# A two-layer MoE behind attention on one core: block 0's load and maximum moved beside the second layer's weights, and a two-instruction activation

## The chip, the cores and the metric

The program runs on one core of a Trainium2 chip. The metric is device microseconds of one execution, lower is better; the time before is the median of three runs. Engines are named as in the profile: PE (TensorE matmuls), PEld (its weight loads), DVE (VectorE), ACT (ScalarE), POOL (GpSimd) and SP (SyncE, which issues every DMA of this kernel).

## The reference, cut to what matters

```python
def _moe_ref(x, w_in, w_out):            # layer 1, after the attention
    h = x @ w_in                         # 1792 x 768 times 768 x 2048
    g = h * (1.0 / (1.0 + np.exp(-1.702 * h)))
    return (g @ w_out).astype(np.float32)

def _moe2_ref(x, w_in, w_out, alpha):    # layer 2
    h = x @ w_in
    g = np.maximum(h, 0.0) + alpha * np.minimum(h, 0.0)
    return (g @ w_out).astype(np.float32)
```

The attention has 4 batches of 12 heads, 448 positions each; its output is the x of layer 1, and y of layer 1 is the x of layer 2. alpha holds 2048 numbers between 0 and 0.3, one for each column of h.

## The kernel before

All large matmuls are done in float16 with each operand split into a high and a low half (three matmuls for one product), so every operand needs a scale, and the scale needs a maximum over the whole tensor or block.

**Layer 1.** Attention and layer 1 are interleaved by batch b = 0 to 3. `moe1(b)` computes 16 blocks `hp` (L672, 18 matmuls each), applies the activation (ACT L680, DVE L681), splits the result into `g` (L124, L125), and `moe1_out` then makes 6 tiles `yp` (L695, 48 matmuls each), which ACT copies to `y` (L703) and SP stores to `y_dram` (L704).

**Weights of layer 2.** While batch 3 runs, `late_weights` steps through `weights(...)`: it loads w_in (`w2raw`), rebuilds its float32 numbers in `w2n` (ACT L132, DVE L148, L149), takes row maxima (L222) and splits the rows into `w2i` (ACT L163, DVE L164). `w2i` lies in the memory of layer 1's `w1i`, which the last `hp` matmul reads. There are four `w2n` tiles for six rows of weights, so the last two rows can be rebuilt only when the first are split. Then the maximum over all rows is taken: `wcol` (L171) on each partition, and `partition_max` across partitions. `partition_max` puts the column on a diagonal (`diag`, L117), multiplies it on PE by a matrix of ones into `pm` (L119), and reduces `pm` on DVE (L120).

**Layer 2.** 1792 tokens are worked in BLOCKS of 512, 512, 512 and 256. `prepare(i)` loads block i of `y_dram` into `yr` (one buffer), takes its maximum (L748), crosses partitions with a `pm` of its own and splits the block into `x2`. `moe2_in(i)` computes 16 blocks `h` (L780, 18 matmuls each), applies the activation and stores `pos` to `g_dram`. Between them `second_out_weights` prepares w_out on ACT and DVE. `token_sums` and `moe2_out` then make the last product (L943).

**What sets the order.** The code issues instructions in one order, and a scheduler with a timeline of its own writes the final order of each engine before the program runs. On the chip each engine works through its own list. `hp`, `yp`, `h` and every `pm` share one PSUM pool, `ps_m`, of three banks, which are also handed out when the order is written. `yr` lies in the pool `p2`, which is opened where the pool `w2s` of the weights was closed. `P0` counts the steps of `late_weights` after which the rest of `prepare(0)` runs; `P1` lists the values of m at which `prepare(i + 1)` goes on.

Of the kernel before, what the change touches and what calls it, by code (L numbers as in the profile page):

```python
# [9 lines left out]
F32 = mybir.dt.float32  # L10
# [3 lines left out]
AF = mybir.ActivationFunctionType  # L14
ALU = mybir.AluOpType
AX = mybir.AxisListType.X
# [29 lines left out]
R1O = 4  # L46
G1I = 1
G1O = 2
P1 = (2, 8)
P0 = 14  # L50
PAIR0 = 44
W2_RAW = 6
RSQRT_SEED = float(0x5F3759DF)
# [3 lines left out]
def attention_moe_kernel(  # L57
# [17 lines left out]
    nc = tc.nc  # L75
# [6 lines left out]
    KD = DM // 128  # L82
    KF = FF // 128
# [3 lines left out]
    const = ctx.enter_context(tc.tile_pool(name="const", bufs=1))  # L87
# [3 lines left out]
    work = ctx.enter_context(tc.tile_pool(name="work", bufs=2))  # L91
# [10 lines left out]
    def pow2floor(dst, src):  # L102

        nc.vector.tensor_scalar(out=dst, in0=src, scalar1=1e-30, scalar2=None, op0=ALU.max)
        nc.vector.tensor_scalar(
            out=dst.bitcast(I32), in0=dst.bitcast(I32), scalar1=EXP_MASK, scalar2=None, op0=ALU.bitwise_and
        )
# [6 lines left out]
    def partition_max(dst, col):  # L114

        diag = small.tile([128, 128], BF16, tag="diag", name="diag", bufs=1)
        nc.vector.tensor_scalar(out=diag, in0=ident, scalar1=col, scalar2=None, op0=ALU.mult)  # L117
        pm = ps_m.tile([128, 128], F32, tag="m", name="pm")
        nc.tensor.matmul(out=pm, lhsT=ones, rhs=diag, start=True, stop=True)  # L119
        nc.vector.tensor_reduce(out=dst, in_=pm, op=ALU.max, axis=AX)  # L120

    def split(dst, src, scale):

        nc.scalar.activation(out=dst[0], in_=src, func=AF.Copy, scale=scale)  # L124
        nc.vector.scalar_tensor_tensor(  # L125
            out=dst[1], in0=src, scalar=scale, in1=dst[0], op0=ALU.mult, op1=ALU.subtract
        )
# [593 lines left out]
    H2 = DM // 2  # L721

    def alpha_scales():

        nalpha = const.tile([128, KF], F32, name="nalpha")
        nc.sync.dma_start(out=nalpha, in_=moe2_alpha.rearrange("(m p) -> p m", p=128))
        am = const.tile([128, 1], F32, name="am")
        nc.vector.tensor_reduce(out=am, in_=nalpha, op=ALU.max, axis=AX, apply_absolute_value=True)
        nc.vector.tensor_scalar(out=am, in0=am, scalar1=1.0, scalar2=None, op0=ALU.max)
        pow2floor(am, am)  # L730
        a2 = const.tile([128, 1], F32, name="a2")
        partition_max(a2, am)
        nc.vector.tensor_scalar(out=nalpha, in0=nalpha, scalar1=-1.0, scalar2=None, op0=ALU.mult)
        ra = const.tile([128, 1], F32, name="ra")
        nc.vector.reciprocal(out=ra, in_=a2)
        return nalpha, a2, ra

    blocks = {}
    w2 = {}

    def prepare(i):

        o, n = BLOCKS[i]
        p2 = w2["p2"]
        yr = p2.tile([128, KD, n], F32, tag="yr", name="yr", bufs=1)
        nc.sync.dma_start(out=yr, in_=y_dram[:, o:o + n].rearrange("(k p) t -> p k t", p=128))
        one = small.tile([128, 1], F32, tag="yone", name="yone")
        nc.vector.tensor_reduce(  # L748
            out=one, in_=yr.rearrange("p k t -> p (k t)"), op=ALU.max, axis=AX, apply_absolute_value=True
        )  # L750
        pow2floor(one, one)
        yield
        my = small.tile([128, 1], F32, tag="my", name="my")
        partition_max(my, one)
        rmy = small.tile([128, 1], F32, tag="rmy", name="rmy")
        nc.vector.reciprocal(out=rmy, in_=my)
        sc = small.tile([128, KD], F32, tag="ysc", name="ysc")
        nc.vector.tensor_scalar(out=sc, in0=scales["w2i"][1], scalar1=rmy, scalar2=None, op0=ALU.mult)
        x2 = [big.tile([128, 2, n], F16, tag="x", name="x2", bufs=NX) for _ in range(KD)]
        for kk in range(KD):  # L760
            split((x2[kk][:, 0], x2[kk][:, 1]), yr[:, kk], sc[:, kk:kk + 1])
        co = const.tile([128, 1], F32, name=f"co{i}")
        nc.vector.tensor_scalar(
            out=co, in0=my, scalar1=scales["w2i"][0], scalar2=2.0 ** -26, op0=ALU.mult, op1=ALU.mult
        )
        blocks[i] = (x2, co)
        yield

    def moe2_in(i, nalpha):

        o, n = BLOCKS[i]
        p2 = w2["p2"]
        w2i = w2["w2i"]
        x2 = blocks[i][0]
        for m in range(KF):
            ps = ps_m.tile([128, n], F32, tag="m", name="h2")
            c = 0
            for kk in range(KD):
                for e, f in ((0, 0), (0, 1), (1, 0)):
                    nc.tensor.matmul(  # L780
                        out=ps, lhsT=w2i[:, kk, e, m * 128:(m + 1) * 128], rhs=x2[kk][:, f], start=(c == 0), stop=(c == 3 * KD - 1)
                    )
                    c += 1
            pos = p2.tile([128, n], F32, tag="pos", name="pos", bufs=3)
            neg = work.tile([128, n], F32, tag="t", name="neg")
            nc.scalar.activation(out=pos, in_=ps, func=AF.Relu)  # L786
            nc.scalar.activation(out=neg, in_=ps, func=AF.Relu, scale=-1.0)  # L787
            nc.vector.scalar_tensor_tensor(  # L788
                out=pos, in0=neg, scalar=nalpha[:, m:m + 1], in1=pos, op0=ALU.mult, op1=ALU.add
            )  # L790
            nc.sync.dma_start(out=g_dram[m * 128:(m + 1) * 128, o:o + n], in_=pos)
            yield
# [173 lines left out]
    def late_weights(ctx, att):  # L966

        att.close()
        with tc.tile_pool(name="w2s", bufs=1) as w2s:

            def w2i():
                if "w2i" not in w2:
                    w2["w2i"] = big.tile([128, KD, 2, FF], F16, tag="w", name="w2i", bufs=2)
                return w2["w2i"]

            yield from weights(
                moe2_w_in, "w2i", w2i, lambda j: w2s.tile([128, FF], F32, tag="num", name="w2n", bufs=4),
                lambda t: w2s.tile([128, 512, 2], I32, tag="raw", name="w2raw", bufs=W2_RAW), 4, W2_RAW, 2.0 ** 13, scales, 2, 4
            )
        w2["p2"] = ctx.enter_context(tc.tile_pool(name="p2", bufs=2))  # L980
        w2["ps"] = ctx.enter_context(tc.tile_pool(name="ps_d", bufs=5, space=bass.MemoryType.PSUM))
        first = prepare(0)
        next(first)
        for _ in range(P0):
            yield
        next(first)
        yield

    def second_layer(late):
        for _ in late:  # L990
            pass
        nalpha, a2, ra = alpha_scales()
        rest = second_out_weights()
        ready = False
        early = token_sums(0)
        step = 0
        for i in range(len(BLOCKS)):
            nxt = prepare(i + 1) if i + 1 < len(BLOCKS) else iter(())
            for m, _ in enumerate(moe2_in(i, nalpha)):
                if m in P1:  # L1000
                    next(nxt, None)
                for _ in range(1 + step % 2):
                    if not ready:
                        ready = next(rest, None) is None and "w2o" in scales
                        if ready:
                            cg = w2["cg"] = const.tile([128, KF], F32, name="cg")
                            nc.vector.tensor_scalar(out=cg, in0=scales["w2o"][1], scalar1=ra, scalar2=None, op0=ALU.mult)
                            nc.vector.tensor_scalar(
                                out=a2, in0=a2, scalar1=scales["w2o"][0], scalar2=2.0 ** 13, op0=ALU.mult, op1=ALU.mult
                            )  # L1010
                if step >= PAIR0:
                    next(early, None)
                step += 1
        for _ in early:
            pass
        obs = w2["p2"].tile([128, 2, 2, 2, H2], F32, tag="yr", name="ob", bufs=1)
        for p in range(NT // 256):
            nxt = token_sums(p + 1)
            next(nxt, None)
            for o, _ in enumerate(moe2_out(p, a2, obs[:, p % 2])):  # L1020
                next(nxt, None)
                next(nxt, None)
            for _ in nxt:
                pass

    if True:
# [51 lines left out]
        steps = attention([4 * P + r for P in range(NP) for r in range(2, 4)])  # L1078
# [26 lines left out]
        for b in range(B):  # L1105
            last = min(NU, 4 * NP * (b + 2)) + LAG
            first = done
# [42 lines left out]
```

## Time and profile before

| | us |
|---|---|
| median of 3 runs | 1219.34 (1214.65 to 1220.08) |
| profiled execution, its own time | 1210.01 |
| its span, first to last instruction | 1208.2 |
| last `hp` matmul of layer 1 ends | 726.91 |
| first `h` matmul of layer 2 starts | 790.06 |

Times within the span count from its start. The profiled execution lies 9.3 us below the median of the runs; 1.8 us of it lie outside the span.

### The profile page before, as it was taken

To read this page: it belongs to the slowest core of one execution; us is meant where nothing else is said; L and a number is where in the kernel's file an instruction comes from. 1 tells how busy PE (TensorE), PEld (TensorE's weight loads), DVE (VectorE), ACT (ScalarE), POOL (GpSimd) and SP (SyncE) were. 2 spreads that over 40 slices of the span, in tenths; PEclk is the share of its full clock that TensorE was granted. 3 is DMA by queue.
4 is the path that set the end of the run, shared out by engine and by line. 5 is a ranking of instruction groups with operands and counts; after the bars stand their busy time and mean duration, and the time that the engine had idled before them with its cause. 6 is when DMAs were issued, how large, how long until landed. Compare 5 with 4: busy or idle time off the path is not lost.

```text
span 1208.2 us, 18626 instructions
## 1 busy us (share of the span) xinstructions
PE 1086.0 (90%) x6829; PEld 610.5 (51%) x6829; DVE 827.2 (68%) x1451; ACT 704.2 (58%) x1447; POOL 138.7 (11%) x236
## 2 busy tenths in 40 slices
PE   0568899868989898999999999799999999999998
PEld 0345577655444444555555545344444467566665
DVE  6999888997555777456751768569895352887451
ACT  3676777877376776567862545237666343665220
POOL 3112000354311513130000000000000000000000
PEclk9878999979999899999999999899999999999999
DMA  7983555577577665666542821364524216244111
GB/s 201 270 213 104 157 134 133 118 149 139 141 150 146 122 146 115 133 123 128 107 88 61 299 92 51 127 251 166 210 79 166 79 66 192 91 148 119 43 27 33
DMA packets 266539, 160.62 MB, mean 133 GB/s; under 512 B 188112, under 2 KB 249808, under 8 KB 266448
## 3 DMA queue, kind: packets, MB, share of 16 engines
q1 hardware_dynamic: 266448, 159.44, 50.3%
q8 instruction: 53, 0.87, 0.3%
q14 instruction: 38, 0.31, 0.1%
HBM read 92.02 MB, written 25.69 MB: 97 GB/s over the span
## 4 chain that ended last, share of the span: by engine, by line
PE 49%; DVE 21%; DMA 12%; ACT 9%; issue 5%; SPq 3%; POOL 0%; DVEq 0%; ACTq 0%
PE op L943 13%; PE yp L695 10%; PE h L780 9%; PE hp L672 7%; PE xp L530 4%; DVE ph L505 3%; ACT pr L461 3%; DMA w2raw<-in_moe_w_in_dram 2%; PE sp L447 2%; DVE nm L452 2%; PE hp L625 2%; DMA vst<-in_v_dram 2%; PE tp L494 2%; DMA yr<-y_dram 1%; DMA w2raw<-in_moe_w_out_dram 1%
## 5 line engine op out<-in xcount | busy, mean ns | idle before, releaser
L695 PE MATMUL yp<-g,w1o 128*128 128x448 f16 x1152 | 229.4, 358 | 4.8 <-DVE g L125 2.6
L780 PE MATMUL h<-x,w2i 128*128 128x512 f16 (+1 forms) x1152 | 219.2, 352 | 3.0 <-ACT neg L787 3.0
L672 PE MATMUL hp<-x,w1i 128*128 128x448 f16 x864 | 169.9, 354 | 2.9 <-DVE t L681 2.9
L695 PEld LDWEIGHTS <-w1o 128*128 128x128 f16 x1152 | 111.5, 99 | 115.7 <-issue 17.7
L780 PEld LDWEIGHTS <-w2i 128*128 128x128 f16 x1152 | 112.6, 98 | 108.5 <-issue 3.7
L505 DVE SCALAR_TENSOR_TENSOR ph<-pr,sm,ph 128x448 f16<-128x448 f32 x126 | 104.9, 857 | 30.9 <-ACT ph L479 30.2
L672 PEld LDWEIGHTS <-w1i 128*128 128x128 f16 x864 | 82.6, 98 | 85.4 <-issue 11.2
L461 ACT ACTIVATE pr<-sp,nm,c_s 128x448 f32<-128x448 f32 x168 | 120.3, 720 | 5.1 <-PE tp L494 3.1
L452 DVE TENSOR_REDUCE nm<-sp 128x2 f32<-128x896 f32 x96 | 92.4, 963 | 8.5 <-PE sp L447 6.4
L479 ACT ACTIVATE ph<-pr,sm 128x448 f16<-128x448 f32 x126 | 78.1, 660 | 22.9 <-DVE sm L470 21.0
L943 PEld LDWEIGHTS <-even 128*128 128x128 f16 x672 | 65.7, 98 | 43.1
L788 DVE SCALAR_TENSOR_TENSOR pos<-neg,nalpha,pos 128x512 f32<-128x512 f32 (+1 forms) x64 | 43.4, 680 | 60.5 <-ACT neg L787 60.3
L447 PE MATMUL sp<-t 64*128 64x448 f16 (+1 forms) x480 | 62.5, 363 | 18.6 <-ACT pr L461 18.6
L625 PE MATMUL hp<-x,w1i 128*128 128x256 f16 (+1 forms) x576 | 64.8, 271 | 11.5 <-DVE t L637 8.0
L786 ACT ACTIVATE pos<-h 128x512 f32<-128x512 f32 (+1 forms) x64 | 34.4, 537 | 67.1 <-PE h L780 58.4
L494 PE MATMUL tp<-dg,pr 128*128 128x128 f32 x336 | 56.1, 326 | 15.4 <-DVE dg L474 14.9
L625 PEld LDWEIGHTS <-w1i 128*128 128x128 f16 x576 | 54.8, 103 | 25.9 <-issue 22.3
L453 ACT ACTIVATE nm<-nm,c_s 128x2 f32<-128x2 f32 x96 | 28.0, 291 | 67.4 <-DVE nm L452 67.3
L943 PEld LDWEIGHTS <-odd 128*128 128x128 f16 x504 | 49.2, 98 | 33.5 <-DVE odd L893 1.1
L943 PE MATMUL op<-w2lo,even 128*128 128x384 f16 x384 | 63.5, 326 | 0.0
L494 PEld LDWEIGHTS tp<-dg,pr 128*128 128x128 f32 x336 | 49.8, 230 | 26.9 <-DVE dg L474 11.8
L125 DVE SCALAR_TENSOR_TENSOR g<-t,ratio_w1o,g 128x448 f16<-128x448 f32 x64 | 45.7, 718 | 18.2 <-ACT g L124 17.9
(202 smaller groups left out, 1620.9 us busy)
## 6 DMA issues: line engine op xcount, KB each, us to landing
g<-in_moe_w_in_dram SPq DMA_DIRECT2D x24, 512.0 KB, 5.0
g<-in_moe_w_out_dram SPq DMA_DIRECT2D x32, 384.0 KB, 3.9
w2raw<-in_moe_w_in_dram SPq DMA_DIRECT2D x24, 512.0 KB, 5.9
w2raw<-in_moe_w_out_dram SPq DMA_DIRECT2D x16, 768.0 KB, 6.4
g_dram<-pos SPq DMA_DIRECT2D x48, 256.0 KB, 2.0
gp<-g_dram SPq DMA_DIRECT2D x8, 1024.0 KB, 6.6
odd<-g_dram SPq DMA_DIRECT2D x6, 1024.0 KB, 5.8
y_dram<-y SPq DMA_DIRECT2D x24, 224.0 KB, 2.4
```

The lines of the kernel that those rows point to most:

```text
L447: nc.tensor.matmul(out=sp[:, j, 0:S] if n == 2 else sp[ds, 0, 0:S], lhsT=qt[ds] if n == 2 else qt[ds, 64:128], rhs=kt[ds, 0:S], start=(i = ...
L452: nc.vector.tensor_reduce(out=nm[:, 0:n], in_=sp[:, 0:n, 0:S], op=ALU.max, axis=AX, negate=True)
L461: nc.scalar.activation(out=pr[i], in_=sp[:, i, 0:S], func=AF.Exp, bias=nm[:, i:i + 1], scale=c_s, accum_out=sm[:, i:i + 1])
L479: nc.scalar.activation(out=ph[:, i, 0:S], in_=pr[i], func=AF.Copy, scale=sm[:, i:i + 1])
L494: nc.tensor.matmul(out=tp[:, c, i], lhsT=pr[i][:, o:o + 128], rhs=ph[:, i], start=True, stop=True)
L505: nc.vector.scalar_tensor_tensor(out=ph[:, i, S:2 * S], in0=pr[i], scalar=sm[:, i:i + 1], in1=ph[:, i, 0:S], op0=ALU.mult, op1=ALU.subtract)
L530: nc.tensor.matmul(out=xp[64 * j:64 * j + 64, t:t + n], lhsT=vs[ks, j, c], rhs=pt[ks, kc, o:o + n], start=(i == 0), stop=(i == len(steps) ...
L625: nc.tensor.matmul(out=ps, lhsT=w1i[:, kk, e, m * 128:(m + 1) * 128], rhs=xs[0, kk][:, f, cols], start=(i == 0), stop=(i == 3 * KD - 1))
L672: nc.tensor.matmul(out=ps, lhsT=w1i[:, kk, e, m * 128:(m + 1) * 128], rhs=x[:, f], start=(n == 0), stop=(n == 3 * KD - 1))
L695: nc.tensor.matmul(out=ps, lhsT=w1o[:, m, e, j * 128:(j + 1) * 128], rhs=g[:, m, f], start=(n == 0), stop=(n == 3 * KF - 1))
L780: nc.tensor.matmul(out=ps, lhsT=w2i[:, kk, e, m * 128:(m + 1) * 128], rhs=x2[kk][:, f], start=(c == 0), stop=(c == 3 * KD - 1))
L943: nc.tensor.matmul(out=ps, lhsT=ops[:, o, m, f], rhs=rhs[:, e], start=(c == 0), stop=(c == 3 * KH - 1))
```

## The change

In layer 2, `yr` gets a pool of its own, `py`, opened as soon as the attention's memory is closed. `prepare(0)` starts there: its load is issued before the weights, its maximum is taken at step 6 of the weights and its `pm` at step 14 (`P0 = (6, 14)`); only the split into `x2` stays behind the weights. `prepare` has more stops, so `P1` has four entries.

The activation changes as well. `sign` is +1 where alpha is at most 1 and -1 elsewhere, `slope` is alpha times sign. ACT writes sign * h, and DVE takes the larger of slope * h and that, reading h from PSUM itself; the sign is multiplied back into `cg`. Before, ACT wrote the relu of h and the relu of -h, and DVE joined the two.

```diff
-P1 = (2, 8)
-P0 = 14
+P1 = (2, 6, 8, 9)
+P0 = (6, 14)
...
-        nalpha = const.tile([128, KF], F32, name="nalpha")
+        slope = const.tile([128, KF], F32, name="slope")
...
+        sign = const.tile([128, KF], F32, name="sign")
+        nc.vector.tensor_scalar(out=sign, in0=slope, scalar1=1.0, scalar2=None, op0=ALU.is_le)
+        nc.vector.tensor_scalar(out=sign, in0=sign, scalar1=2.0, scalar2=-1.0, op0=ALU.mult, op1=ALU.add)
+        nc.vector.tensor_tensor(out=slope, in0=slope, in1=sign, op=ALU.mult)
...
-        nc.vector.tensor_scalar(out=nalpha, in0=nalpha, scalar1=-1.0, scalar2=None, op0=ALU.mult)
...
-        p2 = w2["p2"]
-        yr = p2.tile([128, KD, n], F32, tag="yr", name="yr", bufs=1)
+        yr = w2["py"].tile([128, KD, n], F32, tag="yr", name="yr", bufs=1)
         nc.sync.dma_start(out=yr, in_=y_dram[:, o:o + n].rearrange("(k p) t -> p k t", p=128))
+        yield
...
         nc.vector.reciprocal(out=rmy, in_=my)
+        yield
...
-            neg = work.tile([128, n], F32, tag="t", name="neg")
-            nc.scalar.activation(out=pos, in_=ps, func=AF.Relu)
-            nc.scalar.activation(out=neg, in_=ps, func=AF.Relu, scale=-1.0)
+            nc.scalar.activation(out=pos, in_=ps, func=AF.Copy, scale=sign[:, m:m + 1])
             nc.vector.scalar_tensor_tensor(
-                out=pos, in0=neg, scalar=nalpha[:, m:m + 1], in1=pos, op0=ALU.mult, op1=ALU.add
+                out=pos, in0=ps, scalar=slope[:, m:m + 1], in1=pos, op0=ALU.mult, op1=ALU.max
             )
...
         att.close()
+        w2["py"] = ctx.enter_context(tc.tile_pool(name="py", bufs=1))
+        first = prepare(0)
+        next(first)
...
-            yield from weights(
+            steps = weights(
...
+            for i, _ in enumerate(steps):
+                if i in P0:
+                    next(first)
+                yield
...
-        first = prepare(0)
-        next(first)
-        for _ in range(P0):
-            yield
         next(first)
```

The scheduler wrote a new order on every engine. Three places of it follow.

On PE, at the end of layer 1, the matmul `pm` that carries the maximum of the second layer's weights (its `diag` is made from `wcol`) stood behind three of the six `yp` tiles, `yp_8016` being the third, with 48 matmuls for each tile:

```order
L695 LDWEIGHTS w1o_78
L695 MATMUL yp_8016<-g_7361,w1o_78 128x448
L119 LDWEIGHTS ones_75
L119 MATMUL pm_8034<-diag_8032,ones_75 128x128
L695 LDWEIGHTS w1o_78
L695 MATMUL yp_8094<-g_7361,w1o_78 128x448
```

In the changed program the same `pm` is `pm_7971`, `yp_7921` is the first of the six tiles and `yp_8023` the second:

```order
L695 LDWEIGHTS w1o_78
L695 MATMUL yp_7921<-g_7361,w1o_78 128x448
L119 LDWEIGHTS ones_75
L119 MATMUL pm_7971<-diag_7969,ones_75 128x128
L695 LDWEIGHTS w1o_78
L695 MATMUL yp_8023<-g_7361,w1o_78 128x448
```

So it moved ahead of 96 `yp` matmuls, and 240 now stand behind it. The `pm` of block 0, which stood 48 matmuls after it, now stands between the 8th and the 9th `hp` block of batch 3.

On DVE, in the last units of the attention, the maximum of `yr` and the three instructions that make its `diag` now stand among the instructions of the softmax (`sm`, `ph`, `nm`):

```order
 L452 TENSOR_REDUCE nm<-sp 128x2
 L470 RECIPROCAL sm<-sm 128x2
-L505 SCALAR_TENSOR_TENSOR ph<-pr,sm,ph 128x448 x2
-L452 TENSOR_REDUCE nm<-sp 128x2
+L752 TENSOR_REDUCE yone<-yr 128x1
+L505 SCALAR_TENSOR_TENSOR ph<-pr,sm,ph 128x448 x2
+L452 TENSOR_REDUCE nm<-sp 128x2
+L104 TENSOR_SCALAR yone<-yone 128x1
+L105 TENSOR_SCALAR yone<-yone 128x1
+L117 TENSOR_SCALAR diag<-ident,yone 128x128
 L470 RECIPROCAL sm<-sm 128x2
```

They stood behind the last split of the weights, some 100 rows later.

On DVE again, in block 1 of layer 2, the maximum of `yr` for block 2 stood ahead of the activations of two blocks `h` (the 17th and the 18th):

```order
L105 TENSOR_SCALAR rm_w2o<-rm_w2o 128x1
L748 TENSOR_REDUCE yone<-yr 128x1
L788 SCALAR_TENSOR_TENSOR pos<-neg,nalpha,pos 128x512
L830 TENSOR_SCALAR inv_w2o<-rm_w2o 128x1
L125 SCALAR_TENSOR_TENSOR w2lo<-w2num,inv_w2o,w2lo 128x384
```

Now it stands behind them:

```order
L792 SCALAR_TENSOR_TENSOR pos<-h_8824,slope,pos 128x512
L792 SCALAR_TENSOR_TENSOR pos<-h_8852,slope,pos 128x512
L104 TENSOR_SCALAR rm_w2o<-rm_w2o 128x1
L846 TENSOR_TENSOR w2num<-w2num 128x384
L125 SCALAR_TENSOR_TENSOR w2lo<-w2num,inv_w2o,w2lo 128x384
L752 TENSOR_REDUCE yone<-yr 128x1
```

Two activations, one difference and one split moved ahead of the reduction.

## Rows read from the trace of the kernel before

**Rows 1.** The page's busy times: engine, busy us, share of the span, instructions.

```profile
PE 1086.0 (90%) x6829; PEld 610.5 (51%) x6829; DVE 827.2 (68%) x1451; ACT 704.2 (58%) x1447; POOL 138.7 (11%) x236
```

**Rows 2.** Stretches: PE, PEld, DVE, ACT, POOL busy, granted clock, DMA share, GB/s.

```profile
67.00:408.00 341.00, 289.67 (x2088) 184.23 (x2089) 277.60 (x555) 246.83 (x581) 78.05 (x114) 0.92 0.62 142
...
790.00:1018.00 228.00, 225.02 (x1198) 116.84 (x1197) 153.77 (x267) 129.16 (x236) 0.00 (x0) 1.00 0.42 150
```

**Rows 3.** Timeline of PE, 699 to 826 us: start, us, instructions, [idle before, releaser].

```profile
699.51 27.40 PE L672 MATMUL hp<-x,w1i 128*128 128x448 f16 x144 [2.56 <-DVE t L681]
726.75 27.40 PE L695 MATMUL yp<-g,w1o 128*128 128x448 f16 x144
753.99 0.22 PE L119 MATMUL pm<-diag,ones 128*128 128x128 bf16 x1
...
770.00 0.29 PE L119 MATMUL pm<-diag,ones 128*128 128x128 bf16 x1 [6.70 <-DVE diag L117]
770.08 20.09 PE L695 MATMUL yp<-g,w1o 128*128 128x448 f16 x96
...
790.06 35.13 PE L780 MATMUL h<-x,w2i 128*128 128x512 f16 x162
```

**Rows 4.** Timelines of ACT, DVE and SP between layers, 727 to 770 us.

```profile
727.54 7.67 ACT L163 ACTIVATE w2i<-w2n,inv_w2i 128x2048 f16<-128x2048 f32 x4
...
729.57 9.14 DVE L164 SCALAR_TENSOR_TENSOR w2i<-w2n,inv_w2i,w2i 128x2048 f16<-128x2048 f32 x4 [1.27 <-ACT w2i L163]
...
752.60 0.26 DVE L117 TENSOR_SCALAR diag<-ident,wcol 128x128 bf16<-128x128 bf16 x1
...
759.41 0.37 SPq L746 DMA_DIRECT2D yr<-y_dram  x1
...
765.92 3.35 DVE L748 TENSOR_REDUCE yone<-yr 128x1 f32<-128x3072 f32 x1 [6.01 <-DMA yr<-y_dram]
```

**Rows 5.** Stretches of 2 us after PE's wait, columns as in rows 2.

```profile
770.00:772.00 2.00, 2.00 (x7) 0.87 (x8) 0.84 (x6) 0.81 (x2) 0.00 (x0) 0.50 0.03 8
...
774.00:776.00 2.00, 2.00 (x12) 1.00 (x11) 2.00 (x4) 0.98 (x2) 0.00 (x0) 1.00 0.00 0
```

**Rows 6.** Timeline of DVE, 698 to 701 us: the instructions that free two PSUM banks.

```profile
698.85 0.61 DVE L681 SCALAR_TENSOR_TENSOR t<-t,hp 128x448 f32<-128x448 f32 x1
...
699.98 0.61 DVE L681 SCALAR_TENSOR_TENSOR t<-t,hp 128x448 f32<-128x448 f32 x1
```

**Rows 7.** Loads of yr (tile view), and timelines of SP, DVE, PE late in attention.

```profile
DMA to landing us min/median/max: 6.5/6.8/9.3
...
621.78 0.60 SPq L416 DMA_DIRECT2D vs<-vs  x1
...
627.43 1.28 DVE L505 SCALAR_TENSOR_TENSOR ph<-pr,sm,ph 128x448 f16<-128x448 f32 x2 [0.73 <-ACT ph L479]
...
653.46 1.39 PE L530 MATMUL xp<-pt,vs 128*64 128x256 f16 x22
```

**Rows 8.** Groups by line and shape, 600 to 1020 us: busy us, mean ns, idle before.

```profile
L788 DVE SCALAR_TENSOR_TENSOR pos<-neg,nalpha,pos 128x512 f32<-128x512 f32 x48 | 35.7, 746 | 42.5 <-ACT neg L787 42.5
...
L125 DVE SCALAR_TENSOR_TENSOR g<-t,ratio_w1o,g 128x448 f16<-128x448 f32 x19 | 12.9, 681 | 7.2 <-ACT g L124 7.2
...
L681 DVE SCALAR_TENSOR_TENSOR t<-t,hp 128x448 f32<-128x448 f32 x19 | 11.7, 618 | 10.3 <-ACT t L680 10.3
...
L703 ACT ACTIVATE y<-yp,c_y 128x448 f32<-128x448 f32 x12 | 7.5, 626 | 39.3 <-PE yp L695 18.2 <-issue 12.6 <-PE pm L119 8.4
```

**Rows 9.** PE's waits from 700 us on, and the timeline of DVE, 868 to 909 us.

```profile
PE h L780 <- ACT neg L787: 3.0, 3, 1.6
...
868.26 3.35 DVE L748 TENSOR_REDUCE yone<-yr 128x1 f32<-128x3072 f32 x1 [3.50 <-DMA yr<-y_dram]
...
908.07 0.74 DVE L788 SCALAR_TENSOR_TENSOR pos<-neg,nalpha,pos 128x512 f32<-128x512 f32 x1
```

**Rows 10.** PE's waits, 67 to 408 us: us in total, times, longest.

```profile
PE sp L447 <- ACT pr L461: 17.6, 16, 2.7
```

More of the change, by code (lines that the diff above doesn't have):

```diff
@@ L723, in alpha_scales @@
     def alpha_scales():
-        nalpha = const.tile([128, KF], F32, name="nalpha")
-        nc.sync.dma_start(out=nalpha, in_=moe2_alpha.rearrange("(m p) -> p m", p=128))
+        slope = const.tile([128, KF], F32, name="slope")
+        nc.sync.dma_start(out=slope, in_=moe2_alpha.rearrange("(m p) -> p m", p=128))
         am = const.tile([128, 1], F32, name="am")
-        nc.vector.tensor_reduce(out=am, in_=nalpha, op=ALU.max, axis=AX, apply_absolute_value=True)
+        nc.vector.tensor_reduce(out=am, in_=slope, op=ALU.max, axis=AX, apply_absolute_value=True)
+        sign = const.tile([128, KF], F32, name="sign")
+        nc.vector.tensor_scalar(out=sign, in0=slope, scalar1=1.0, scalar2=None, op0=ALU.is_le)
+        nc.vector.tensor_scalar(out=sign, in0=sign, scalar1=2.0, scalar2=-1.0, op0=ALU.mult, op1=ALU.add)
+        nc.vector.tensor_tensor(out=slope, in0=slope, in1=sign, op=ALU.mult)
         nc.vector.tensor_scalar(out=am, in0=am, scalar1=1.0, scalar2=None, op0=ALU.max)
@@ L732, in alpha_scales @@
         partition_max(a2, am)
-        nc.vector.tensor_scalar(out=nalpha, in0=nalpha, scalar1=-1.0, scalar2=None, op0=ALU.mult)
         ra = const.tile([128, 1], F32, name="ra")
         nc.vector.reciprocal(out=ra, in_=a2)
-        return nalpha, a2, ra
+        return sign, slope, a2, ra
     blocks = {}
@@ L767, in prepare, with moe2_in @@
         yield
-    def moe2_in(i, nalpha):
+    def moe2_in(i, sign, slope):
         o, n = BLOCKS[i]
@@ L991, in second_layer @@
             pass
-        nalpha, a2, ra = alpha_scales()
+        sign, slope, a2, ra = alpha_scales()
         rest = second_out_weights()
@@ L998, in second_layer @@
             nxt = prepare(i + 1) if i + 1 < len(BLOCKS) else iter(())
-            for m, _ in enumerate(moe2_in(i, nalpha)):
+            for m, _ in enumerate(moe2_in(i, sign, slope)):
                 if m in P1:
@@ L1007, in second_layer @@
                             nc.vector.tensor_scalar(out=cg, in0=scales["w2o"][1], scalar1=ra, scalar2=None, op0=ALU.mult)
+                            nc.vector.tensor_tensor(out=cg, in0=cg, in1=sign, op=ALU.mult)
                             nc.vector.tensor_scalar(
@@ L1015, in second_layer @@
             pass
-        obs = w2["p2"].tile([128, 2, 2, 2, H2], F32, tag="yr", name="ob", bufs=1)
+        obs = w2["py"].tile([128, 2, 2, 2, H2], F32, tag="yr", name="ob", bufs=1)
         for p in range(NT // 256):
```

## The prediction

> **What bounds the kernel now.** The page comes first: PE is busy 90% of the span [rows 1], so time is won or lost where PE is not busy. The stretches show where that is: PE misses 51 us between 67 and 408 us, but only 3.0 between 790 and 1018 [rows 2]. The hand-over between the layers is read from the timeline of PE [rows 3]. The last `hp` matmul ends at 726.91 (699.51 + 27.40); then come 144 `yp` matmuls at 190 ns (27.40 / 144), the `pm` of the weights without a wait, 48 more `yp`, a wait of 6.70 us for the `diag` of block 0, and 96 `yp`. The first `h` starts at 790.06, 63.15 us after the last `hp`.
>
> That wait has a plain cause. `yr` can only be loaded at 759.41, when the last split of the weights frees the memory; the reduction waits 6.01 us for the load and takes 3.35 us [rows 4]. All the while 96 `yp` matmuls, which need nothing of it, stand behind the `pm` on PE: one waiting matmul holds all that stand behind it. The reader should keep this for the next part.
>
> **The change, part by part.**
>
> *The old wait goes.* With `yr` loaded and reduced before the weights, the `pm` of block 0 has its `diag` long before PE comes to it. Removed: 6.70 us of waiting, and the slow matmuls behind it. [...] That is 1.8 us, 8.5 in all.
>
> *A new wait comes.* The new order puts the `pm` of the weights behind 48 `yp` matmuls and not behind 144. What it waits for doesn't become earlier. Its `diag` is made from `wcol`, the maximum over all six rows of weights. Rows 5 and 6 need a `w2n` tile that rows 1 and 2 give back when they are split, and the splits write `w2i` in the memory of `w1i`, which the last `hp` matmul reads. So the chain starts when `hp` ends: ACT's four splits at 727.54, DVE's four until 738.71, and at the far end the `diag` at 752.60, done at 752.86 [rows 4]. From the end of `hp` that is 26.0 us; PE ran the `pm` at 753.99 [rows 3], just after it. In the new order PE has 48 x 190 ns = 9.1 us of work for these 26.0 us and then stands still, some 17 us. Inside the chain the last L681 of layer 1 goes in front of DVE's rebuilding (0.6 us), while ACT's splits start 0.5 us earlier, since L680 goes behind them; I take these as even.
>
> After the `pm` PE has 240 `yp` left: 45.7 us, plus 1.8 us for a clock at 0.50 when it resumes, as after the old wait; I have no row for a stall twice as long just here, so I let it cost as much. From the end of `hp` to the first `h`: 26.0 + 0.15 for the `pm` + 45.7 + 1.8 = 73.7 us, where it was 63.15. **+10.5 us.** The loads of w_out wait for the memory of `g`, so for the last `yp`; they move along with `h`, and nothing catches up there.
>
> *A bank.* The `pm` of block 0 now stands between the 8th and 9th `hp`, where PE already waited 2.56 us for one of three banks [rows 3]. The bank that L681 frees at 699.46 goes to the `pm`, and the 9th `hp` takes the one freed at 700.59 [rows 6]: **+1.1 us**, and `hp` ends so much later. Nothing at all if DVE comes earlier to these two; 3.3 (three times as much) if the `pm` keeps its bank over two more blocks.
>
> *The reduction in the attention.* In the order DVE comes to it at the L505 of 627.43. The load can start once SP has issued the attention's last load of `vs`, at 622, and takes 6.5 to 9.3 us [rows 7], so the reduction may end at 632 to 635 and the softmax units behind it run some 5 to 8 us late. PE meets the last but one of them at 653.46, 26 us after that L505 [rows 7], filled until there with `yp` of batch 2. I take nothing; bounds 0 and 3 us.
>
> *Activation.* ACT's second instruction goes, 64 times. ACT is not what PE waits for in this stage save 3.0 us in three waits [rows 9]. The new copy with a scale on each partition is nearest to L703, 626 ns for 448 columns [rows 8]. The product on DVE reads h from PSUM: L681 does so for 448 columns in 618 ns, L125 of the same size reads memory alone in 681 [rows 8], so I take 63 ns off the 746 of L788, 3 us over the 48 large blocks; bounds 0 and 3. [...]
>
> But the bank of an `h` block is now held until DVE has multiplied, no longer only until ACT has read it. With three banks, block m + 3 cannot start before the product of block m is done. A block takes 3.9 us (35.13 / 9), and DVE lags: the product of block 26 starts at 908.07 and ends some 0.7 later [rows 9], while without any wait block 29 would start at 790.06 + 29 x 3.88 + 0.2 = 902.8. On the old order that is a wait of 5.9 us. In the new one the reduction of block 2, which idled DVE for 3.50 us [rows 9], has two products and two more instructions in front of it, some 2.4 us of work that now fills the idle time; the load it waits for hardly moves. With that and 27 x 0.06 = 1.6 us from the shorter products, 1.9 us are left; the reduction still ends late, and I take 3.0, as much as PE waits there now: **net 0**, bounds -3.0 and +2.9 (5.9 - 3.0).
>
> *Small.* Three DVE instructions more for `sign` and `slope`, one less, one more for `cg`: under 0.5 us.
>
> *The order before 408 us.* The new DVE instructions at about 70 us shuffled all queues from there to 408 us. Work and units are the same; one score group moved behind 90 `yp` matmuls. PE waits there in small pieces, 16 for ACT with a longest of 2.7 us [rows 10]. No reason favours a sign: 0, bounds -6 and +6 (two of those longest waits gone or come).
>
> Sum: 10.5 + 1.1 + 0 + 0 = **+11.6 us**. The profiled time would go from 1210.01 to about 1222. The runs stood 9.3 us above it, which I leave as it is: 1219.3 + 11.6 = **1231 us**.
>
> **The rivals.**
>
> *The hand-over becomes free.* If the `pm` of the weights found its `diag` ready, the old 8.5 us would be won and only the bank paid: 1219.3 - 8.5 + 1.1 = 1212. For it speaks that the scheduler placed it there, so its own timeline had the maximum early. Against it speaks the chain: `diag` must come within 9.1 us of the end of `hp`, and the eight splits alone last until 738.71, 11.8 us after it. It decides where 17 us of the chain can vanish. Chance 0.08.
>
> *DVE holds the banks.* If the products lag as on the old order, or more, PE waits 5.9 to 9 us in blocks 14 to 29 where it waited 3.0: +11.6 + 2.9 to 6, 1234 to 1237. For it: DVE is the late one through this stage. Against it: it has less to do, and the reduction moved. [...] Chance 0.12.
>
> *The early order decides.* If the shuffle before 408 us gives 6 us back, the result is 1225, within half a per cent; if it costs 6, 1237. Chance 0.14, half each way.
>
> *Forecast*, with its parts within their bounds: 0.66, its own range 1226 to 1236.
>
> **How the numbers follow.** Slower or faster by 0.5% (6.1 us) is about what a measurement of this kernel can tell from no change. Slower: 0.63 of the forecast, the banks' 0.12, half of the early order (0.04 counted, since 1237 needs the rest as forecast): 0.79. Within: 0.03 of the forecast and most of the other half, 0.12. Faster: the free hand-over and a little, 0.09. The range leaves out most of the free hand-over below and the sum of two dear cases above: 1217 to 1239.
>
> **What the profile would show.** Right: on PE a wait of 16 to 18 us for DVE's `diag` right after the first 48 `yp`, a clock of 0.50 after it, 240 `yp` in one piece, and 73 to 75 us from the last `hp` to the first `h`; the old wait gone; `yr` reduced before 640 us. PE's waits in the `h` stage would name DVE's product, 2 to 5 us together, and ACT's waits would be gone. Wrong: a wait before that `pm` of under 8 us, or an end of `hp` more than 6 us from 728, or waits over 9 us in the `h` stage.

## The result: 11 us slower, and where they went

| | before | changed |
|---|---|---|
| median of 11 runs, us | 1214.31 | 1225.39 (1221.99 to 1230.86) |
| ratio | | 1.0102 (1.0084 to 1.0121) |
| profiled execution | 1210.01 | 1230.82 |
| last `hp` ends | 726.91 | 738.22 |
| last `hp` to first `h` | 63.15 | 73.44 |
| first `h` to end of the last `h` | 227.5 | 226.9 |

The change costs 11.1 us between the medians; 11.6 was forecast. The level of before came down by 5 us with more runs, and with it the time itself: 1214.3 + 11.6 is 1225.9. The 1231 that was named is 5.6 too high, 5.0 of it for that reason, and 1225.39 lies just below the 1226 to 1236 of the forecast taken alone. The two profiled executions differ by more, 20.8 us, since the one of before lies 4.3 us below its median and the one of the change 5.4 above its own. The changed one is 7.4 us late when the `hp` of batch 3 begin, loses 3.9 in them and 10.3 in the hand-over, and wins 0.6 in `h`. So stages are compared below, and over several profiles where they scatter.

The page first, the busy times, as in [rows 1]:

```profile
PE 1088.6 (89%) x6829; PEld 611.2 (50%) x6829; DVE 823.3 (67%) x1454; ACT 683.2 (56%) x1383; POOL 142.2 (12%) x236
```

ACT has 64 instructions less and 21 us less work, and PE did not gain from it. The timeline of PE from the bank of block 0's `pm` to the first `h`, which answers to [rows 3]:

```profile
708.01 0.22 PE L119 MATMUL pm<-diag,ones 128*128 128x128 bf16 x1 [1.78 <-DVE t L681]
...
709.14 29.08 PE L672 MATMUL hp<-x,w1i 128*128 128x448 f16 x144 [0.92 <-DVE t L681]
...
738.06 8.68 PE L695 MATMUL yp<-g,w1o 128*128 128x448 f16 x45
750.72 0.35 PE L695 MATMUL yp<-g,w1o 128*128 128x448 f16 x1 [3.98 <-ACT g L124]
753.83 0.90 PE L695 MATMUL yp<-g,w1o 128*128 128x448 f16 x2 [2.76 <-DVE g L125]
764.35 0.27 PE L119 MATMUL pm<-diag,ones 128*128 128x128 bf16 x1 [9.62 <-DVE diag L117]
764.41 47.36 PE L695 MATMUL yp<-g,w1o 128*128 128x448 f16 x240
811.61 0.22 PE L119 MATMUL pm<-diag,ones 128*128 128x128 bf16 x1
811.66 35.13 PE L786 MATMUL h<-x,w2i 128*128 128x512 f16 x162
```

The old wait of 6.70 us is gone, and 16.4 us stand in its place (3.98 + 2.76 + 9.62). They end where the `diag` of the weights comes. The rows of ACT and DVE that lead to it, as in [rows 4]:

```profile
738.26 7.68 ACT L163 ACTIVATE w2i<-w2n,inv_w2i 128x2048 f16<-128x2048 f32 x4 [1.35 <-PE hp L672]
740.29 9.14 DVE L164 SCALAR_TENSOR_TENSOR w2i<-w2n,inv_w2i,w2i 128x2048 f16<-128x2048 f32 x4 [2.67 <-ACT w2i L163]
745.85 0.61 ACT L680 ACTIVATE t<-hp,c_t 128x448 f32<-128x448 f32 x1
...
764.04 0.25 DVE L117 TENSOR_SCALAR diag<-ident,wcol 128x128 bf16<-128x128 bf16 x1
```

The chain is as long as before: its `diag` is done at 764.29, 26.1 us after the last `hp` (738.22), where it was 26.0. Only the work that stood in front of the `pm` became less. The reader should also see the L680 at 745.85: the activation of the last `hp` block stands behind the four splits, so the last three matmuls of the first `yp` tile wait for it too. That takes nothing more here, since PE would have stood still until 764.35 anyway.

The granted clock after the wait, in stretches of 2 us, as in [rows 5]:

```profile
766.00:768.00 2.00, 2.00 (x7) 0.79 (x6) 1.98 (x1) 2.00 (x2) 0.00 (x0) 0.50 0.00 0
768.00:770.00 2.00, 2.00 (x12) 0.99 (x11) 2.00 (x2) 2.00 (x4) 0.00 (x0) 0.99 0.00 0
```

In the `h` stage PE's waits are as long as before, 3.0 us, and have another name, as an answer to [rows 9]:

```profile
PE h L786 <- DVE pos L792: 2.1, 2, 1.8
PE h L786 <- DVE rm_w2o L104: 0.9, 1, 0.9
```

### The profile page after: what moved, and what is told of

Its sections match the earlier page's. It is cut to its first block, busy times and chain, and to the rows that moved or that the text cites. A ratio compares the mean times of both kernels' runs of the same rounds, so it can differ in the third digit from the quotient of the medians.

```text
span 1229.0 us, 18563 instructions
## 1 busy us (share of the span) xinstructions
PE 1088.6 (89%) x6829; PEld 611.2 (50%) x6829; DVE 823.3 (67%) x1454; ACT 683.2 (56%) x1383; POOL 142.2 (12%) x236
## 4 chain that ended last, share of the span: by engine, by line
PE 57%; DVE 18%; DMA 10%; ACT 7%; issue 4%; SPq 4%; POOL 1%; ACTq 0%; DVEq 0%; POOLq 0%
PE op L947 16%; PE yp L695 14%; PE h L786 10%; PE hp L672 7%; PE xp L530 4%; PE sp L447 3%; ACT pr L461 2%; PE tp L494 2%; DMA w2raw<-in_moe_w_in_dram 2%; DVE nm L452 2%; PE hp L625 1%; DVE ph L505 1%; DMA qk<-in_q_dram 1%; DMA w2raw<-in_moe_w_out_dram 1%; DVE g L125 1%
## 5 line engine op out<-in xcount | busy, mean ns | idle before, releaser
L672 PE MATMUL hp<-x,w1i 128*128 128x448 f16 x864 | 173.9, 359 | 4.3 <-DVE t L681 3.6
L505 DVE SCALAR_TENSOR_TENSOR ph<-pr,sm,ph 128x448 f16<-128x448 f32 x126 | 98.1, 807 | 26.1 <-ACT ph L479 26.0
L791 ACT ACTIVATE pos<-h,sign 128x512 f32<-128x512 f32 (+1 forms) x64 | 40.1, 629 | 84.8 <-PE h L786 79.2
L792 DVE SCALAR_TENSOR_TENSOR pos<-h,slope,pos 128x512 f32<-128x512 f32 (+1 forms) x64 | 43.4, 680 | 61.6 <-ACT pos L791 61.6
L625 PE MATMUL hp<-x,w1i 128*128 128x256 f16 (+1 forms) x576 | 63.3, 268 | 11.1 <-DVE mx_w1o L120 3.5
L494 PE MATMUL tp<-dg,pr 128*128 128x128 f32 x336 | 56.1, 328 | 16.5 <-DVE dg L474 16.4
L125 DVE SCALAR_TENSOR_TENSOR g<-t,ratio_w1o,g 128x448 f16<-128x448 f32 x64 | 49.1, 768 | 17.0 <-ACT g L124 16.7
```

Of the source, the lines that this page charges most:

```text
L125: nc.vector.scalar_tensor_tensor(out=dst[1], in0=src, scalar=scale, in1=dst[0], op0=ALU.mult, op1=ALU.subtract)
L494: nc.tensor.matmul(out=tp[:, c, i], lhsT=pr[i][:, o:o + 128], rhs=ph[:, i], start=True, stop=True)
L505: nc.vector.scalar_tensor_tensor(out=ph[:, i, S:2 * S], in0=pr[i], scalar=sm[:, i:i + 1], in1=ph[:, i, 0:S], op0=ALU.mult, op1=ALU.subtract)
L625: nc.tensor.matmul(out=ps, lhsT=w1i[:, kk, e, m * 128:(m + 1) * 128], rhs=xs[0, kk][:, f, cols], start=(i == 0), stop=(i == 3 * KD - 1))
L672: nc.tensor.matmul(out=ps, lhsT=w1i[:, kk, e, m * 128:(m + 1) * 128], rhs=x[:, f], start=(n == 0), stop=(n == 3 * KD - 1))
```

## Experiments

The theory on trial was the prediction's (A below): all of the loss is the place of the weights' `pm`, and a little the bank. But the order alone doesn't say why the scheduler put it there. The code does, in lines that the diff passes by:

```python
            if hold and j == hold:
                yield "held"           # weights(): ahead of the splits
...
        if hold:
            yield "rows"               # weights(): ahead of the maximum
...
                    for _ in range(1 if i < 2 * KF else 2):
                        if got is None or i >= 2 * KF:
                            got = next(late, None)
```

The loop over batch 3 stops stepping when it gets anything but None, until the last `hp` is issued. `yield from weights(...)` handed these two words on; the new loop ends in a bare `yield`, which hands on None. Of the two only "held" can hold the loop: counting the steps, "rows" comes when i is past 2 * KF, where the loop steps whatever it got. So the splits and the maximum are issued earlier in the program, and the scheduler, which goes by that order, wrote the `pm` ahead of two `yp` tiles.

### Either half alone

`act_alone` is before with the new activation; `prep_alone` is the changed kernel with the old one. Of each diff only lines of the activation are shown:

```diff
 act_alone, against before
...
+            nc.scalar.activation(out=pos, in_=ps, func=AF.Copy, scale=sign[:, m:m + 1])
...
+                out=pos, in0=ps, scalar=slope[:, m:m + 1], in1=pos, op0=ALU.mult, op1=ALU.max
...
 prep_alone, against the changed kernel
...
-            nc.scalar.activation(out=pos, in_=ps, func=AF.Copy, scale=sign[:, m:m + 1])
+            nc.scalar.activation(out=pos, in_=ps, func=AF.Relu)
+            nc.scalar.activation(out=neg, in_=ps, func=AF.Relu, scale=-1.0)
...
```

> The kernel before with the new activation alone (sign, slope, copy, maximum); prepare and the hand-over stay as they were. Theory A, the prediction's: the loss sits in the hand-over, so this stays within 3 us of before, near 1214, with 63 us from the last hp to the first h, and 228 us for the h stage with 2 to 4 us of PE waiting for DVE's product. Rival B: the order before 408 us, which the new DVE instructions of alpha shuffle, costs the 7 us that the two profiles differ by at 408 us; then this stands 5 to 7 us above before, near 1220.

> The changed kernel with the old activation (two relus and a join): only block 0's load, maximum and pm are moved. Theory A: the whole loss, 73 us from the last hp to the first h (10 more than before) and some 4 us more for the bank of pm between the hp blocks, so 1224 to 1228. Rival B: the hand-over loses 10 us but the early order keeps the place it had, so 1218 or less, as the early order carried the rest.

`act_alone`: 1214.65 us, ratio 1.0017 (0.9999 to 1.0035); 63.5 us from `hp` to `h`, 227.5 us of `h`, 3.7 of them PE's waits for DVE. `prep_alone`: 1224.41 us, ratio 1.0105 (1.0074 to 1.0135); 72.9 us to the first `h`, 227.5 us of `h`. The loss goes with the moved `prepare`, and theory A stands. Rival B keeps 0.9 us between the medians (1213.79 for before in these runs), 2 by the ratio and at most 4 by its interval. The 4 us expected for the bank don't show in `prep_alone`: its `hp` of batch 3 took 58.3 us, those of `act_alone` 58.6. PE in `prep_alone` waits as in the changed kernel:

```profile
743.86 0.53 PE L695 MATMUL yp<-g,w1o 128*128 128x448 f16 x1 [3.98 <-ACT g L124]
746.98 0.90 PE L695 MATMUL yp<-g,w1o 128*128 128x448 f16 x2 [2.58 <-DVE g L125]
757.43 0.27 PE L119 MATMUL pm<-diag,ones 128*128 128x128 bf16 x1 [9.55 <-DVE diag L117]
```

### The word back

```diff
-            for i, _ in enumerate(steps):
+            for i, mark in enumerate(steps):
                 if i in P0:
                     next(first)
-                yield
+                yield mark
```

> The changed kernel with one word back: late_weights hands on what weights yields, so that its stops named held and rows hold the loop again until the last hp, as before. The pm of the weights then stands behind three yp tiles. Theory A (the place of that pm is the cost): it finds its diag ready 26 us after the last hp, no wait, 55 us from the last hp to the first h, 18 less than the changed kernel; the bank wait between the hp blocks stays, some 4 us; 1208 to 1211. Rival C (the moved load and maximum themselves delay the weights' chain on DVE and SP): the diag comes later than 30 us after the last hp, PE still waits 5 us or more at that pm, 63 us or more to the first h, 1214 or above.

1207.85 us, ratio 0.9953 (0.9935 to 0.9971), just below theory A's range. PE's timeline:

```profile
703.51 0.22 PE L119 MATMUL pm<-diag,ones 128*128 128x128 bf16 x1 [1.94 <-DVE t L681]
704.65 28.69 PE L672 MATMUL hp<-x,w1i 128*128 128x448 f16 x144 [0.92 <-DVE t L681]
733.17 27.40 PE L695 MATMUL yp<-g,w1o 128*128 128x448 f16 x144
760.41 0.22 PE L119 MATMUL pm<-diag,ones 128*128 128x128 bf16 x1
760.47 27.40 PE L695 MATMUL yp<-g,w1o 128*128 128x448 f16 x144
...
787.76 12.46 PE L786 MATMUL h<-x,w2i 128*128 128x512 f16 x57
```

No wait from the last `hp` to the first `h`, 54.4 us (733.33 to 787.76), 19.0 less than in the changed kernel. The `diag` stands at 759.46 in this trace and is done 26.4 us after the last `hp`: the moved load and maximum do not delay the chain, so rival C falls. The moved `prepare` was worth its 8.7 us (63.15 - 54.4); the lost word took them and 10.3 more. Around the bank PE waited 2.9 us, not 4.

### The place alone

The stops stay lost, and empty steps move the maximum back behind three tiles:

```diff
-            for i, _ in enumerate(steps):
+            for i, mark in enumerate(steps):
...
+                if mark == "rows":
+                    for _ in range(LATER):      # LATER = 16
+                        yield
```

> The changed kernel, stops still lost, but 16 empty steps stand ahead of the maximum of the weights, which puts its pm behind three yp tiles again. Theory A (the place of that pm is the cost): 54 to 56 us from the last hp to the first h and the time of the kernel with the word back, 1206 to 1210. Rival E (what the word brought back is the hour at which the splits and the last two rows are issued, and the pm's place only followed): PE still waits 6 us or more in the hand-over, and the time is above 1214.

1209.64 us, ratio 0.9968 (0.9956 to 0.9981), 54.4 us to the first `h`:

```profile
732.37 27.40 PE L696 MATMUL yp<-g,w1o 128*128 128x448 f16 x144
759.61 0.22 PE L120 MATMUL pm<-diag,ones 128*128 128x128 bf16 x1
759.67 27.40 PE L696 MATMUL yp<-g,w1o 128*128 128x448 f16 x144
```

Rival E falls: with the place of the `pm` back, the wait is gone though the word is still lost. The splits are still issued early, and the last L680 (L681 here, all lines being one further down) still stands behind them, as in the changed kernel:

```profile
732.57 7.68 ACT L164 ACTIVATE w2i<-w2n,inv_w2i 128x2048 f16<-128x2048 f32 x4 [1.36 <-PE hp L673]
740.16 0.61 ACT L681 ACTIVATE t<-hp,c_t 128x448 f32<-128x448 f32 x1
...
757.59 0.25 DVE L118 TENSOR_SCALAR diag<-ident,wcol 128x128 bf16<-128x128 bf16 x1
```

The chain is nearly as long, too: the `diag` is done 25.3 us after the last `hp` (757.84 - 732.53). So neither the hour of the splits nor the place of L680 makes PE wait; the place of the `pm` does.

### The bank of block 0's `pm`

```diff
-P0 = (6, 14)
+P0 = (6, 20)      # mark_pm_late, against mark_back; (6, 34) in changed_pm_late, against the changed kernel
```

> As the one before, and the pm of block 0 is issued six steps later (20 for 14), which puts it among the first yp matmuls and no longer between two hp blocks. Theory A: the 4 us of bank waits between the hp blocks fall back to the 2.6 of before, so the last hp ends some 3.5 us earlier and the whole is 1205 to 1207. Rival D (those waits are DVE's lateness and not the bank of pm): they stay, and the time is that of the kernel with the word back within 1 us.

> The changed kernel with the pm of block 0 issued at step 34 for 14, so that it stands among the first yp tile; the pm of the weights stays behind 48 yp matmuls. The hand-over should keep its 73 us. If the pm between the hp blocks costs what the two kernels with the word back differ by, 5 us, this gives 1219 to 1222; if it costs only the bank wait that the profiles of those two show, 1 us, 1223 to 1226.

`mark_pm_late` came to 1202.71 us, 5.1 below `mark_back`, below what was expected. `changed_pm_late` came to 1225.26, 0.1 below the changed kernel, with 73.8 us in the hand-over. The two pairs did not agree, so the first was run again:

> The kernel with the word back, once more, for the 5 us that the place of block 0's pm seemed to be worth in one pair of kernels and not at all in the other. Theory F (the pm between the hp blocks costs about 1 us, the rest was the scatter of executions in the stages before): 1206 to 1209, and 1 to 2 us above its partner. Rival G (it costs 5 us where the hand-over is free): 4 to 6 us above its partner.

> The kernel with the word back and block 0's pm among the yp tiles, once more. Theory F: 1204 to 1207, with 58 to 59 us from the first hp of the last batch to the last, 1 us less than its partner. Rival G: 1201 to 1204.

1206.33 and 1204.78 us: 1.6 apart, theory F. The profiles agree: from the first `hp` of batch 3 to the end of the last it takes 58.3, 59.3, 59.4, 59.4 and 61.3 us in the five profiles with the `pm` between the blocks (mean 59.5), and 57.1 to 59.0 in the seven without (mean 58.1). So the `pm` between the blocks costs some 1.4 us, and the two groups overlap. `mark_pm_late` shows the waits that are left when it is gone, both for a bank and both without a `pm`:

```profile
693.86 6.97 PE L672 MATMUL hp<-x,w1i 128*128 128x448 f16 x36 [1.68 <-DVE t L681]
702.60 27.40 PE L672 MATMUL hp<-x,w1i 128*128 128x448 f16 x144 [1.77 <-DVE t L681]
```

They are 3.4 us together, more than the 2.9 of `mark_back`: rival D is right that the waits stay. Over the stage PE waits 3.2 us on average with the `pm` between the blocks and 3.2 without. What differs is the work. In four of the five profiles with it the 9th block took 4.9 to 5.3 us from its first matmul to the end of its last, where every other block took 3.6; `prep_alone` is the one where the 9th took 3.6 as well. In the changed kernel the granted clock fell to 0.50 behind the two waits:

```profile
710.00:712.00 2.00, 2.00 (x7) 0.76 (x5) 2.00 (x2) 0.64 (x1) 0.00 (x0) 0.50 0.91 258
```

### The early order

`pm_late_old_activation` is `mark_pm_late` with the two relus, and so with the early order of before; `before_again` is before unchanged.

> The fastest kernel so far (word back, pm of block 0 among the yp tiles) with the old activation, and so with the order before 408 us of the kernel before. Theory A (the activation is worth nothing here): 227.5 us of h stage, and 1201 to 1205, as with the new one. Rival B (the new early order, which stood 5 us later at 289 us in all four profiles that have it, costs some of that for good): 1197 to 1200.

> The kernel before once more, for a second profile. If the 5 us at 289 us belong to the new order, this stands at 283 to 284 us there again; if they are the scatter of executions, anywhere up to 289. The time should lie in the range of its runs, 1209 to 1220.

`pm_late_old_activation`: 1205.53 us, ratio 0.994 (0.9918 to 0.9963), 226.7 us of `h`; that is 0.5 above theory A's range. `before_again`: 1217.47 us in its one run, with 64.6 us from `hp` to `h`. Count PE's matmuls: behind the first 1432 the orders agree again, and the next one, of a block of layer 1, comes at 281.3 to 284.6 us in the four profiles with the old order, at 286.6 to 289.8 in the eight with the new one. The two groups don't overlap, so the 5.3 us between their means are no scatter. But on average they are given back. Stretches with equal counts of PE's matmuls, of `pm_late_old_activation`:

```profile
67.00:281.30 214.30, 180.41 (x1332) 128.20 (x1333) 197.79 (x420) 163.85 (x385) 35.66 (x54) 0.92 0.59 142
281.30:462.20 180.90, 157.87 (x1071) 79.80 (x1069) 121.24 (x200) 118.16 (x275) 57.72 (x80) 0.95 0.66 136
```

and of `mark_pm_late`:

```profile
67.00:287.20 220.20, 180.05 (x1333) 127.80 (x1334) 197.38 (x426) 167.36 (x391) 40.11 (x55) 0.92 0.57 139
287.20:460.40 173.20, 154.86 (x1070) 78.17 (x1068) 115.27 (x197) 114.92 (x268) 55.29 (x79) 0.97 0.70 141
```

The one is 5.9 us late at first and takes 7.7 less for the next 1071. Over all twelve profiles the 2500th matmul stands at 460.8 us with the old order and 460.7 with the new, in single profiles at 457 to 464. The first two profiles are no example of it: the changed kernel is 5.8 us late at the first point, and 7.4 from the 2600th matmul up to batch 3. What sets the pace between the two points was not tried. Rival B falls: its 1197 to 1200 did not come.

## Why the prediction was right, point by point

**The old wait goes** (8.5 us). Right: with the new wait away too, `hp` to `h` falls from 63.15 to 54.4, by 8.7. Of the 8.5, 1.8 are the slow matmuls: the 96 `yp` behind the wait took 20.09 us [rows 3], where 96 x 190 ns are 18.3, and the granted clock stood at 0.50 when PE resumed and at 1.00 from 774 on [rows 5]. The other two profiles with the old hand-over have 63.45 and 64.62.

**A new wait comes** (+10.5). Right, term by term: the `pm` ran 26.1 us after the last `hp` (26.0 forecast), 240 `yp` took 47.36 us (45.7 + 1.8 forecast), 73.44 us in all (73.7 forecast), 10.3 more than before; over three profiles of each hand-over 73.4 stand against 63.7, 9.6 more. The wait was to be some 17 us in one piece; 16.4 came in three. That the last L680 behind the splits would stop three matmuls of the first tile wasn't seen, and cost nothing as long as `diag` came last. The prediction took the place of the `pm` from the order and didn't ask why it was there; the lost word "held" is the answer, and with it a gain of 6 to 7 us was to be had (`mark_back`, in its two measurements).

**A bank** (+1.1). The size came out, 1.4 on average over twelve profiles, and by luck. The wait for the second bank is there, 0.92 us, but PE's waits over the whole stage are no longer for it. The 1.4 are slow matmuls: 1.1 us on average in the 9th block, and the `pm` itself. The prediction took a slower clock into account behind the two long waits and not behind this one. In the changed kernel's own profile the stage is 3.9 us longer than in the profile of before, beyond the bound of 3.3: 1.8 of it are waits, which scatter in all profiles (2.2 to 4.4 us), and 1.7 the slow 9th block.

**The reduction in the attention** (0). Right. The load left at 629.4 us and DVE ended the reduction before 640, each later than forecast (622, and 632 to 635) by about what the whole execution was late by then. PE meets the unit behind it 7.4 us later than in [rows 7], as late as it had been since its 2600th matmul, at 485 us:

```profile
636.27 3.35 DVE L752 TENSOR_REDUCE yone<-yr 128x1 f32<-128x3072 f32 x1 [2.69 <-DMA yr<-y_dram]
...
660.88 1.39 PE L530 MATMUL xp<-pt,vs 128*64 128x256 f16 x22
```

**Activation** (net 0). The sum was right, 3.0 us of waits before and after, and one term was not. The product on DVE was to be 63 ns shorter; by line and shape it reads:

```profile
L792 DVE SCALAR_TENSOR_TENSOR pos<-h,slope,pos 128x512 f32<-128x512 f32 x48 | 35.7, 745 | 38.3 <-ACT pos L791 38.3
L791 ACT ACTIVATE pos<-h,sign 128x512 f32<-128x512 f32 x48 | 32.5, 680 | 61.2 <-PE h L786 55.6 <-DMA g_dram<-pos 5.6
```

745 ns, where L788 took 746 [rows 8]: the 63 ns did not come. My two rows behind the 63 ns differed in more than where they read: L125 wrote float16, and took its scalar from a column with one number for each partition; L681 wrote float32, with the constant 1.0 for a scalar. Two more groups of before, of 512 columns and reading memory alone, speak for the scalar:

```profile
L125 DVE SCALAR_TENSOR_TENSOR x<-yr,ysc,x 128x512 f16<-128x512 f32 x18 | 12.4, 745 | 0.8 <-ACT x L124 0.8
...
L149 DVE SCALAR_TENSOR_TENSOR w2n<-w2raw,w2n 128x512 int32<-128x512 int32 x24 | 15.8, 685 | 0.1
```

The first writes float16 and takes no less than L788 and L792, which have a column for a scalar as well; the second has a constant and takes 60 ns less. It works on int32, so this is a likely reason and not a shown one.

The product of block 26 starts 115.0 us after the first `h` (926.71 less 811.66), 118.0 before: 3.0 us earlier of the 4.0 that were counted on. None of it comes from the products. DVE's idle time before the reduction of block 2, 3.50 us before, is now nearly filled:

```profile
888.55 3.35 DVE L752 TENSOR_REDUCE yone<-yr 128x1 f32<-128x3072 f32 x1 [0.33 <-DMA yr<-y_dram]
```

**The order before 408 us** (0, with 6 either way). Right in the sum: `act_alone` is 0.9 us above before between the medians, 2 by a ratio whose interval begins at 0.9999. In part this was luck: the new order does cost 5.3 us on the way, near the bound of 6, and a stretch behind it gives them back for a cause that stays open.

**The rivals.** "The hand-over becomes free" was the one that one word decides: with it, 7.4 us less than before were to be expected (8.5 less the bank's 1.1), and `mark_back` gained 5.9 and 7.2 in its two measurements. "DVE holds the banks" did not come in any kernel: 226.7 to 228.4 us of `h` in all profiles, whichever the activation. No run shows the 6 us at the upper end of its sum: PE's waits in `h` were 3.0 us before and 3.0 in the changed kernel.

**A version that beats both.** The word back and block 0's `pm` at step 20: 1202.71 and 1204.78 us, ratios 0.9915 (0.9888 to 0.9941) and 0.9924 (0.9901 to 0.9948) to before, some 20 us below the changed kernel.

## What to carry to other kernels

A wait that is removed can come back at the matmul beside it: compare what stands in front of each waiting instruction with how long its chain takes from a fixed event, here 9.1 us of work for a chain of 26. When a generator that hands on values is wrapped in a loop, its values are part of the schedule: a bare `yield` in place of `yield from` moved a matmul past 96 others. And two profiles that differ by 7 us in an early stage say little by themselves: over twelve of them the order cost 5 us there and on average gave them back, which the first two did not show.

## What the runs showed of the hardware

The `SCALAR_TENSOR_TENSOR` of 128 x 512 float32 takes 745 ns with one operand in PSUM and 746 with both in memory, each with a scalar for every partition. ACT's copy of 512 columns from PSUM takes 680 ns with a scale for each partition, where a relu with none took 589 and one with a constant scale 590: the new activation saves ACT 0.5 us for each block, not the half.

PE's clock was granted at 0.50 after the wait of 6.70 us and after the 16.4 us alike, and stood at 0.99 or 1.00 some 4 us later in both: the longer wait cost no more behind it (1.7 us, and 1.8 behind the shorter). In the changed kernel it also fell to 0.50 behind two short waits, 1.78 us and 0.92 with one `pm` between them. Behind such a pair, 1.8 to 2.1 us and 0.9, one block of 18 matmuls was slower by 1.3 to 1.7 us in four of five profiles. Behind the single wait of 2.56 us in before the clock stayed at 1.00, from 699.5 to 705.5 us.
